# A fused top-k attention and two feed-forward stages on one core: GpSimd's elementwise work handed to ScalarE and VectorE, and another set of expert products beside the attention

## Chip, core and metric

One core of a Trainium2 chip runs the whole program. The metric is the device time of one execution in microseconds (us). The engines are called as the profile calls them: PE (TensorE's matmuls) and PEld (its weight loads), DVE (VectorE), ACT (ScalarE), POOL (GpSimd) and SP (SyncE, whose queue issues every DMA here). They run side by side, each through its own instructions in a fixed order, and wait for one another through semaphores.

## What is computed

```python
scores = (q @ k.T) / sqrt(64)            # 2 batches, 8 heads, 576 x 576
scores = where(scores >= 32nd largest of the row, scores, -1e9)
x  = softmax(scores) @ v                 # rearranged to 1152 x 512
h  = x @ w_in;  x1 = (h * sigmoid(h)) @ w_out          # 512 -> 2048 -> 512
P  = exp(x1 @ w_gate - max), 8 times scaled to row sums 1 and column sums N/8
out = sum over 8 experts e of P[:, e] * (relu(x1 @ w1[e]) @ w2[e])   # 512 -> 1024 -> 512
```

`w_in` and `w_out` arrive as 64-bit floats and are narrowed on the chip.

## The kernel before

The 1152 tokens are nine row tiles of 128. The attention is worked off as 72 score tiles (128 rows by 576 columns; 64 of one head, 8 that hold the last 64 rows of two heads). For each, `score_tile` (L283) makes the scores on PE, ACT copies them out of PSUM (L293), DVE finds the 32 largest with four `max` and three `match_replace` passes (L301, L307), ACT takes the exponential (L305), DVE masks and sums (`scalar_tensor_tensor`, L310) and inverts the sum (L312, L313), POOL multiplies the row by the inverse (L314), and PE transposes the result (L317, L319). `av` (L322) then multiplies by `v`.

Five groups of row tiles follow each other: tile 0; 1 and 2; 3 and 4; 5 and 6; 7 and 8. As soon as the attention of group 0, 1 or 2 is done, its rows go through the first feed-forward stage (m0, m1, m2) while DVE goes on with the attention of later groups. Tile 0 does so in `row_ffn` (L489): plain float32 matmuls with the activations as the stationary operand and 512 weight columns moving. Groups 1 and 2 do so in `ffn` and `step` (L428, L378), in 16 chunks of 128 hidden columns: each float32 operand is split in a high and a low part, and a product is three matmuls (`mm3`, L134). A chunk's weights are two 128x512 blocks, loaded by SP's queue and split by ACT and POOL in `load_split` (L527, the split itself at L127 and L128). A chunk's silu in `step` is: ACT takes tanh from PSUM (L403) and copies the PSUM tile (`hs`, L406), POOL multiplies and adds (L407, L408), makes the high part (L421) and the low part (L422). PE multiplies these by `w_out` two chunks later (depth 2).

What PE does besides, while the attention runs, is set by the table `FILL` (L24): expert products of row tiles whose x1 is known. After m0 these are experts 0 to 4 of tile 0 ("rows": `row_ffn` in float32, 8 hidden and 8 output matmuls and 8 transposes each). After m1 they are expert 0 of tiles 1 and 2 ("half": the second product in float32) and expert 1 of the same tiles (alternately "split" and "half"), and after m2 expert 0 of tiles 3 and 4 ("split"). Their results are parked in DRAM (`kept_y`).

After the attention, m3 takes the four tiles 5 to 8 together, then come the gate's logits, the eight rounds of scaling (on DVE), and the expert loop: `ORDER` says 7 down to 0, `left[e]` are the tiles of expert e that `FILL` has not done, and `units_of` (L783) cuts them in units of up to four tiles. `weighted` (L761) adds y times P to the accumulator.

The order of the instructions on each engine is not written by hand: the layer below builds a schedule from priorities (`tc.cur_priority`): attention first, then m0 to m2, `FILL` last. SBUF is handed out in stacks; where a new pool reuses memory, each of its tiles waits for the last use of what lay there. On one such stack `first_blocks` (L456) puts the 32 narrowed blocks of `w_in` and `w_out` (`wf`), one buffer each, and the rings of expert weights and of raw blocks (`raw`) come to lie on them when m0 is done.

Of the kernel before, what the change touches and what calls it, by code (L numbers as in the profile page):

```python
# [8 lines left out]
F32 = mybir.dt.float32  # L9
# [3 lines left out]
AF = mybir.ActivationFunctionType  # L13
ALU = mybir.AluOpType
# [3 lines left out]
P = 128  # L18
# [3 lines left out]


FILL = {  # L24
    0: [(e, [0], "rows") for e in range(5)],
    1: [(0, [1, 2], "half"), (1, [1, 2], "split+half")],
    2: [(0, [3, 4], "split")],
}

ORDER = [7, 6, 5, 4, 3, 2, 1, 0]  # L30
# [32 lines left out]
def topk_attention_moe_sinkhorn_kernel(  # L63
# [12 lines left out]
    nc = tc.nc  # L76
# [3 lines left out]
    DFF = w_in.shape[1]  # L80
# [3 lines left out]
    NTT = NT // P  # L84
# [3 lines left out]
    W = DM  # L88
# [26 lines left out]
    kept_y = {}  # L115
# [9 lines left out]
    def split(dH, dL, src, eng=nc.gpsimd):  # L125

        nc.scalar.activation(dH, src, AF.Copy)  # L127
        eng.tensor_sub(dL, src, dH.bitcast(F32))  # L128
# [154 lines left out]
    def score_tile(nm, qq, qL, kk, heads, cols):  # L283

        ps = ps_s.tile([P, 2, 512], F32, name=f"ps_{nm}", tag="s")

        for j in heads:
            for part, a in enumerate((qq, qL)):
                for hh in range(2):
                    nc.tensor.matmul(ps[:, hh, 0:SH], a[:, j, cols], kk[:, j, hh * SH : (hh + 1) * SH],  # L290
                                     start=j == heads[0] and part == 0, stop=j == heads[-1] and part == 1)
        s = sp.tile([P, S], F32, name=f"s_{nm}", tag="s", bufs=SB)
        nc.scalar.activation(s.rearrange("p (a c) -> p a c", a=2), ps[:, :, 0:SH], AF.Copy)  # L293
        w = sp.tile([P, S], F32, name=f"w_{nm}", tag="w")
        m8 = small.tile([P, TOPK], F32, name=f"m8_{nm}", tag="m8")
        sm = small.tile([P, 4], F32, name=f"sm_{nm}", tag="sm")
        e = sp.tile([P, S], F32, name=f"e_{nm}", tag="e")
        src = s
        for r in range(TOPK // 8):
            mr = m8[:, 8 * r : 8 * r + 8]  # L300
            nc.vector.max(mr, src)  # L301
            if r == 0:

                nc.vector.tensor_scalar(sm[:, 0:1], m8[:, 0:1], -SCALE, None, op0=ALU.mult)
                nc.scalar.activation(e, s, AF.Exp, scale=SCALE, bias=sm[:, 0:1])  # L305
            if r < TOPK // 8 - 1:
                nc.vector.match_replace(out=w, in_to_replace=mr, in_values=src, imm_value=-3e38)  # L307
                src = w

        nc.vector.scalar_tensor_tensor(s, s, m8[:, TOPK - 1 : TOPK], e, op0=ALU.is_ge, op1=ALU.mult,  # L310
                                       accum_out=sm[:, 1:2])
        nc.vector.tensor_scalar(sm[:, 2:3], sm[:, 1:2], 1e-9, None, op0=ALU.add)  # L312
        nc.vector.reciprocal(sm[:, 3:4], sm[:, 2:3])  # L313
        nc.gpsimd.tensor_scalar(s, s, sm[:, 3:4], 1.0, op0=ALU.mult, op1=ALU.mult)  # L314
        pt = ps_t.tile([P, 4, P], F32, name=f"pt_{nm}", tag="tr")
        for c in range(4):
            nc.tensor.transpose(pt[:, c, :], s[:, c * P : (c + 1) * P], ident)  # L317
        pt2 = ps_t.tile([P, P], F32, name=f"pt2_{nm}", tag="tr")
        nc.tensor.transpose(pt2, s[:, S - P : S], ident)  # L319
        return pt, pt2  # L320
# [57 lines left out]
    def step(pend, nm, xs, ys, wa, wb, first, last, silu, ph, pool, late=False, depth=2, done=None, half=False):  # L378


        N = len(ys) * P
        ph = ph[:, :N]
        hidden(ph, wa, xs)
        if half:

            gH = pool.tile([P, N], F32R, name=f"gH_{nm}", tag="gH", bufs=depth + 2).bitcast(F32)
            kept = tc.cur_priority
            tc.cur_priority = uid() * 100
            nc.scalar.activation(gH, ph, AF.Relu)
            tc.cur_priority = kept  # L390
            pend.append((ys, wb, gH, None, first, last, done))
            if len(pend) > depth:
                flush(pend)
            return
        gH = pool.tile([P, N], F32R, name=f"gH_{nm}", tag="gH", bufs=depth + 2)
        gL = pool.tile([P, N], F32R, name=f"gL_{nm}", tag="gL", bufs=depth + 2)
        kept = tc.cur_priority
        tc.cur_priority = uid() * 100
        if silu:

            g = hp.tile([P, W], F32, name=f"g_{nm}", tag="g")[:, :N]
            t = hp.tile([P, W], F32, name=f"t_{nm}", tag="t")[:, :N]
            nc.scalar.activation(t, ph, AF.Tanh, scale=0.5)  # L403
            if not late:
                hs = pool.tile([P, N], F32, name=f"hs_{nm}", tag="hs")
                nc.scalar.activation(hs, ph, AF.Copy)  # L406
                nc.gpsimd.tensor_mul(t, t, hs)  # L407
                nc.gpsimd.tensor_add(g, t, hs)  # L408
            else:
                nc.vector.scalar_tensor_tensor(g, t, 1.0, ph, op0=ALU.add, op1=ALU.mult)  # L410
            if late:
                nc.scalar.activation(gH, g, AF.Copy)
                nc.vector.tensor_sub(gL, g, gH.bitcast(F32))
        elif late:
            nc.scalar.activation(gH, ph, AF.Relu)  # L415
            nc.vector.scalar_tensor_tensor(gL, ph, 0.0, gH.bitcast(F32), op0=ALU.max, op1=ALU.subtract)  # L416
        else:
            g = hp.tile([P, W], F32, name=f"g_{nm}", tag="g")[:, :N]
            nc.scalar.activation(g, ph, AF.Relu)
        if not late:  # L420
            nc.gpsimd.tensor_scalar(gH, g, 1.0, 0.0, op0=ALU.mult, op1=ALU.add)  # L421
            nc.gpsimd.tensor_sub(gL, g, gH.bitcast(F32))  # L422
        tc.cur_priority = kept
        pend.append((ys, wb, gH, gL, first, last, done))
        if len(pend) > depth:
            flush(pend)
# [29 lines left out]
    def first_blocks():  # L456


        got = []
        for i in range(2 * DFF // P):  # L460
            tc.cur_priority = conv_at(i)
            F, part, c = i // (2 * NDC), i // NDC % 2, i % NDC
            r = slice(c * P, (c + 1) * P) if part == 0 else slice((F * NDC + c) * P, (F * NDC + c + 1) * P)
            cols = slice(F * W, (F + 1) * W) if part == 0 else slice(0, W)
            x = cvp.tile([P, W], F32, name=f"wf_{i}", tag=f"wf{i}", bufs=1)
            if w_in.dtype == F32:
                nc.sync.dma_start(x, (w_in, w_out)[part][r, cols])
            else:
                raw = cvp.tile([P, W], w_in.dtype, name=f"wfr_{i}", tag="raw")
                nc.sync.dma_start(raw, (w_in, w_out)[part][r, cols])  # L470
                narrow(x, raw, f"{i}")
            got.append(x)
            tc.cur_priority = keep_at(i)
            nc.sync.dma_start(kept_out[r] if part else kept_in[F, c], x)
        return lambda F: (got[2 * NDC * F : 2 * NDC * F + NDC], got[2 * NDC * F + NDC : 2 * NDC * (F + 1)])
# [142 lines left out]
    got = {0: load(units[0]), 1: load(units[1])}  # L618
    qs = turn(units[0], got[0])
    for u, unit in enumerate(units):  # L620
        g = unit[0]
# [18 lines left out]
        if g == 0:  # L640
# [6 lines left out]
            late = right.enter_context(tc.tile_pool(name="late", bufs=1, side="right", reuse_waits="tile"))  # L647
# [106 lines left out]

    last = {}
    left = {e: [tt for tt in range(NTT) if (e, tt) not in kept_y] for e in range(NE)}
    for e in ORDER:
        for tt in left[e]:
            last[tt] = e

    def weighted(e, tt, y):  # L761

        p_ = pr[:, tt, e : e + 1]
        if e == ORDER[0]:

            nc.scalar.activation(acc[:, tt, :], y, AF.Copy)
            return
        o = acc[:, tt, :]
        if last[tt] == e:
            o = x1p.tile([P, DM], F32, name=f"o_{tt}", tag="x1")  # L770
        nc.vector.scalar_tensor_tensor(o, y, p_, acc[:, tt, :], op0=ALU.mult, op1=ALU.add)
        if last[tt] == e:
            for p0, n, dst in out_rows(tt):
                nc.sync.dma_start(dst, o[p0 : p0 + n, :])
# [20 lines left out]
    for i, e in enumerate(ORDER):  # L795
        tc.cur_priority = (300 + i) * GAP
        if i == 1:
            while pend:
                flush(pend)
            for tt in range(NTT):  # L800
                nc.gpsimd.tensor_scalar(acc[:, tt, :], acc[:, tt, :], pr[:, tt, ORDER[0] : ORDER[0] + 1], 1.0,
                                        op0=ALU.mult, op1=ALU.mult)
            for ek, tt in kept_y:
                yk = x1p.tile([P, DM], F32, name=f"yk_{ek}_{tt}", tag="x1")
                nc.sync.dma_start(yk, kept_y[ek, tt])
                weighted(ek, tt, yk)
# [43 lines left out]
```

## Time and profile before

| | us |
|---|---|
| three timed runs: median (lowest to highest) | 1353.98 (1350.36 to 1355.71) |
| the profiled execution | 1354.5 |
| its span, first to last instruction | 1352.7 |
| PE busy in the span | 1247.3 (92%) |
| DVE busy | 734.8 (54%) |
| ACT busy | 515.8 (38%) |
| POOL busy | 446.0 (33%) |

The mean granted clock of PE is 0.962 of its full 2.4 GHz. Busy time counts an engine's instructions, not its waiting; matmuls overlap, so the time between the starts of two of them says more of their cost than their length does. The shares are means over stages that differ: in the stage up to about 545 us attention and feed-forward work lie side by side, and after it PE works through m3 and the expert loop.

### The profile page before, as it was taken

Reading aid. Unit: us, or ns where it says so; the run is one execution under the profiler, and the core shown is the slowest. Engines: PE = TensorE matmul, PEld = TensorE weight load, DVE = VectorE, ACT = ScalarE, POOL = GpSimd, SP = SyncE. Lnnn points to the kernel's source line nnn. Section 1 sums busy time; section 2 is a strip of 40 time slices with the busy share of each in tenths; the row PEclk is TensorE's granted clock in tenths of the full one; section 3 lists DMA queues with packets and bytes.
Section 4 is the critical chain, followed back from the end, with each engine's and each line's share of the span. In section 5 each row is a group of like instructions: output and inputs, shape, how many; then the busy total and the mean of one; then the engine's idle time right before and its main releaser. Section 6 shows DMA issues by size and latency. Waiting matters only on the chain.

```text
span 1352.7 us, 18344 instructions
## 1 busy us (share of the span) xinstructions
PE 1247.3 (92%) x6467; PEld 992.8 (73%) x6467; DVE 734.8 (54%) x1585; ACT 515.8 (38%) x1045; POOL 446.0 (33%) x469
## 2 busy tenths in 40 slices
PE   3568799998899868999999999999999999999998
PEld 2444455676677646888798898898888888888887
DVE  6999999999999936234435312322314223133232
ACT  4766445576557535444412311312213113122221
POOL 2654110599658997613101300200202002011110
PEclk7669899999999988999999999999999999999999
DMA  6998876654345332344302300301302104012210
GB/s 154 287 321 253 268 250 208 186 147 115 100 137 155 90 97 72 113 122 126 108 1 86 110 0 31 95 8 32 94 0 78 47 1 124 0 63 79 63 32 31
DMA packets 154700, 144.89 MB, mean 107 GB/s; under 512 B 34032, under 2 KB 113008, under 8 KB 154608
## 3 DMA queue, kind: packets, MB, share of 16 engines
q1 hardware_dynamic: 154608, 143.72, 35.5%
q8 instruction: 51, 0.84, 0.3%
q14 instruction: 41, 0.34, 0.1%
HBM read 119.03 MB, written 13.63 MB: 98 GB/s over the span
## 4 chain that ended last, share of the span: by engine, by line
PE 68%; DVE 14%; DMA 6%; issue 4%; POOL 4%; ACT 2%; SPq 1%; DVEq 0%; POOLq 0%; ACTq 0%
PE h L137 9%; PE h L136 9%; PE h L135 9%; PE y L135 8%; PE y L136 8%; PE y L137 8%; DVE m L301 5%; DVE w L307 5%; PE bank L497 3%; PE bank L504 2%; DMA wfr<-in_moe_w_in_dram 2%; DVE s L310 2%; PE bank L137 2%; PE bank L136 1%; PE bank L135 1%
## 5 line engine op out<-in xcount | busy, mean ns | idle before, releaser
L416 DVE SCALAR_TENSOR_TENSOR gL<-h,gH 128x512 fp32r<-128x512 f32 (+2 forms) x152 | 88.9, 585 | 311.2 <-ACT gH L415 311.0
L415 ACT ACTIVATE gH<-h 128x512 fp32r<-128x512 f32 (+2 forms) x152 | 78.1, 514 | 425.5 <-PE h L137 422.8
L128 POOL TENSOR_TENSOR wc<-raw,wc 128x512 fp32r<-128x512 f32 x40 | 52.0, 1300 | 452.3 <-ACT wc L127 445.8
L128 POOL TENSOR_TENSOR wa<-raw,wa 128x512 fp32r<-128x512 f32 x96 | 128.6, 1340 | 127.7 <-ACT wa L127 120.6
L301 DVE MAX8 m<-w 128x8 f32<-128x576 f32 x192 | 139.3, 744 | 0.2
L136 PE MATMUL h<-x1L,wc 128*128 128x512 f32 (+2 forms) x380 | 132.7, 349 | 0.0
L137 PE MATMUL h<-x1H,wc 128*128 128x512 f32 (+2 forms) x380 | 132.7, 349 | 0.0
L135 PE MATMUL h<-x1H,wc 128*128 128x512 f32 (+2 forms) x380 | 132.3, 348 | 0.0
L135 PE MATMUL y<-wc,gH 128*128 128x512 f32 x305 | 119.5, 392 | 0.0
L136 PE MATMUL y<-wc,gH 128*128 128x512 f32 x305 | 119.4, 391 | 0.0
L137 PE MATMUL y<-wc,gL 128*128 128x512 f32 x305 | 109.4, 391 | 0.0
L307 DVE MATCH_REPLACE8 w<-m,w 128x576 f32<-128x576 f32 x128 | 94.4, 738 | 0.0
L314 POOL TENSOR_SCALAR s<-s,sm 128x576 f32<-128x576 f32 x64 | 50.9, 795 | 120.5 <-DVE sm L313 78.9
L128 DVE TENSOR_TENSOR wc<-raw,wc 128x512 fp32r<-128x512 f32 x40 | 50.0, 1251 | 69.0 <-ACT wc L127 69.0
L127 ACT ACTIVATE wb<-raw 128x512 fp32r<-128x512 f32 x84 | 53.0, 631 | 71.7 <-PE y L137 23.6
L137 PE MATMUL h<-x1H,wa 128*128 128x512 f32 (+2 forms) x228 | 80.0, 351 | 0.0
L135 PE MATMUL h<-x1H,wa 128*128 128x512 f32 (+2 forms) x228 | 79.8, 350 | 0.0
L136 PE MATMUL h<-x1L,wa 128*128 128x512 f32 (+2 forms) x228 | 79.7, 350 | 0.0
L135 PEld LDWEIGHTS h<-x1H,wc 128*128 128x128 f32 x380 | 71.5, 188 | 10.5
L136 PEld LDWEIGHTS h<-x1L,wc 128*128 128x128 f32 x380 | 71.5, 188 | 10.4
L137 PEld LDWEIGHTS h<-x1H,wc 128*128 128x128 f32 x380 | 71.5, 188 | 8.3
L136 PE MATMUL y<-wb,gH 128*128 128x512 f32 x183 | 72.5, 396 | 0.0
(226 smaller groups left out, 3028.0 us busy)
## 6 DMA issues: line engine op xcount, KB each, us to landing
raw<-in_moe_w_dram SPq DMA_DIRECT2D x164, 256.0 KB, 3.0
raw<-kept_in SPq DMA_DIRECT2D x48, 256.0 KB, 2.9
raw<-kept_out SPq DMA_DIRECT2D x48, 256.0 KB, 2.7
wa<-in_moe_w_dram SPq DMA_DIRECT2D x20, 512.0 KB, 5.4
wb<-in_moe_w_dram SPq DMA_DIRECT2D x20, 512.0 KB, 4.9
wfr<-in_moe_w_in_dram SPq DMA_DIRECT2D x16, 512.0 KB, 5.4
wfr<-in_moe_w_out_dram SPq DMA_DIRECT2D x16, 512.0 KB, 5.8
kept_in<-wf SPq DMA_DIRECT2D x16, 256.0 KB, 5.3
```

Of the source, the lines that this page charges most:

```text
L127: nc.scalar.activation(dH, src, AF.Copy)
L128: eng.tensor_sub(dL, src, dH.bitcast(F32))
L135: nc.tensor.matmul(ps, wH, xH, start=first, stop=False)
L136: nc.tensor.matmul(ps, wH, xL, start=False, stop=False)
L137: nc.tensor.matmul(ps, wL, xH, start=False, stop=last)
L301: nc.vector.max(mr, src)
L307: nc.vector.match_replace(out=w, in_to_replace=mr, in_values=src, imm_value=-3e38)
L310: nc.vector.scalar_tensor_tensor(s, s, m8[:, TOPK - 1 : TOPK], e, op0=ALU.is_ge, op1=ALU.mult, accum_out=sm[:, 1:2])
L314: nc.gpsimd.tensor_scalar(s, s, sm[:, 3:4], 1.0, op0=ALU.mult, op1=ALU.mult)
L415: nc.scalar.activation(gH, ph, AF.Relu)
L416: nc.vector.scalar_tensor_tensor(gL, ph, 0.0, gH.bitcast(F32), op0=ALU.max, op1=ALU.subtract)
L497: nc.tensor.matmul(y, gT[:, c * P : (c + 1) * P], b[c], start=F == 0 and c == 0, stop=F == nF - 1 and c == NDC - 1)
```

## The change

It has four parts.

- In `score_tile`, ACT multiplies the row by the inverse of its sum (an `activation` with a scale per partition) in POOL's place.
- In `step`, silu is one `scalar_tensor_tensor` on DVE, (tanh + 1) times the PSUM tile, for every group; the copy `hs` and POOL's multiplication and addition are gone. The high part is made by ACT (`split`), the low part stays on POOL.
- `FILL` is another table: after m0 experts 0 to 5 of tile 0, after m1 expert 6 of tile 0 and expert 0 of tiles 1 and 2 ("split"), after m2 expert 7 of tile 0. The mode "half" is used no more. Ten products are parked where eleven were; the expert loop has tiles 1 to 8 in units of 4 and 4 for experts 7 to 1, and tiles 3 to 8 in units of 2 for expert 0. The accumulator of tile 0 begins with the first parked product.
- `first_blocks` hands out the 32 blocks in reverse, block 31 first.

```diff
 FILL = {
-    0: [(e, [0], "rows") for e in range(5)],
-    1: [(0, [1, 2], "half"), (1, [1, 2], "split+half")],
-    2: [(0, [3, 4], "split")],
+    0: [(e, [0], "rows") for e in range(6)],
+    1: [(6, [0], "rows"), (0, [1, 2], "split")],
+    2: [(7, [0], "rows")],
 }
@@ score_tile
-        nc.gpsimd.tensor_scalar(s, s, sm[:, 3:4], 1.0, op0=ALU.mult, op1=ALU.mult)
+        nc.scalar.activation(s, s, AF.Copy, scale=sm[:, 3:4])
@@ step
             nc.scalar.activation(t, ph, AF.Tanh, scale=0.5)
-            if not late:
-                hs = pool.tile([P, N], F32, name=f"hs_{nm}", tag="hs")
-                nc.scalar.activation(hs, ph, AF.Copy)
-                nc.gpsimd.tensor_mul(t, t, hs)
-                nc.gpsimd.tensor_add(g, t, hs)
-            else:
-                nc.vector.scalar_tensor_tensor(g, t, 1.0, ph, op0=ALU.add, op1=ALU.mult)
-            if late:
-                nc.scalar.activation(gH, g, AF.Copy)
-                nc.vector.tensor_sub(gL, g, gH.bitcast(F32))
+            nc.vector.scalar_tensor_tensor(g, t, 1.0, ph, op0=ALU.add, op1=ALU.mult)
+            split(gH, gL, g, nc.vector if late else nc.gpsimd)
...
             nc.scalar.activation(g, ph, AF.Relu)
-        if not late:
-            nc.gpsimd.tensor_scalar(gH, g, 1.0, 0.0, op0=ALU.mult, op1=ALU.add)
-            nc.gpsimd.tensor_sub(gL, g, gH.bitcast(F32))
+            split(gH, gL, g)
@@ first_blocks
-        got = []
+        got = [cvp.tile([P, W], F32, name=f"wf_{i}", tag=f"wf{i}", bufs=1) for i in reversed(range(nb))][::-1]
...
-            x = cvp.tile([P, W], F32, name=f"wf_{i}", tag=f"wf{i}", bufs=1)
+            x = got[i]
@@ weighted
-        if e == ORDER[0]:
+        if e == ORDER[0] and tt in left[e]:
             nc.scalar.activation(acc[:, tt, :], y, AF.Copy)
             return
+        if tt not in begun:
+            begun.add(tt)
+            nc.gpsimd.tensor_scalar(acc[:, tt, :], y, p_, 1.0, op0=ALU.mult, op1=ALU.mult)
+            return
```

What this makes of the order is shown at three places. In the rows, `wa`, `wb` and `wf` are weights, `x1H` and `x1L` the parts of x1, `bank` the PSUM banks of the work beside the attention.

The first is PE at the last three score tiles of the attention (`pt_4_1_3_...`). Before, expert 0 of tiles 3 and 4 lies around them (`gL_e_3`, then the next chunk's hidden matmuls):

```order
L317 MATMUL pt_1_3_1_0_6135<-ident,s_1_3_1_0_6116 128x128 x4
L319 MATMUL pt_4_1_3_1_0_6140<-ident,s_1_3_1_0_6116 128x128
L137 MATMUL bank_132<-wb_4615,gL_e_3_0_4637 128x512
L137 MATMUL bank_133<-wb_4615,gL_e_3_0_4637 128x512
L135 MATMUL bank_134<-x1H,wa_4670 128x256
L136 MATMUL bank_134<-x1L,wa_4670 128x256
```

With the change the float32 output matmuls of expert 7 (`gT_e_1`) end ahead of them, and the gate's logits follow (`wgH`, `wgL`):

```order
L319 MATMUL pt_4_1_3_0_1_5739<-ident,s_1_3_0_1_5715 128x128
L488 MATMUL bank_132<-wb_4496,gT_e_1_4516 128x512 x2
L488 MATMUL bank_132<-wb_4497,gT_e_1_4516 128x512 x2
L317 MATMUL pt_1_3_1_0_5767<-ident,s_1_3_1_0_5748 128x128 x4
L319 MATMUL pt_4_1_3_1_0_5772<-ident,s_1_3_1_0_5748 128x128
L571 MATMUL bank_134<-ident,lt_5822 128x8 x4
L317 MATMUL pt_1_3_1_1_5800<-ident,s_1_3_1_1_5781 128x128 x4
L319 MATMUL pt_4_1_3_1_1_5805<-ident,s_1_3_1_1_5781 128x128
L135 MATMUL bank_134<-x1H,wgH 8x128
```

Behind the last score tile stood 60 hidden and 36 output matmuls of expert 0 and all the logits of tiles 0 to 4; of these only the 12 logit matmuls of tile 4 are left there.

The second place is a chunk of m2. Before, POOL has its silu in four steps among the scalings of score tiles (L314) and the weight splits (L128):

```order
L421 TENSOR_SCALAR gH_m_1_4029<-g_m_1_4031 128x256
L408 TENSOR_TENSOR g_m_2_4064<-t_m_2_4065,hs_m_2_4067 128x256
L128 TENSOR_TENSOR wb_4119<-raw_4124,wb_4119 128x512
L422 TENSOR_TENSOR gL_m_1_4030<-g_m_1_4031,gH_m_1_4029 128x256
L421 TENSOR_SCALAR gH_m_2_4062<-g_m_2_4064 128x256
L407 TENSOR_TENSOR t_m_3_4104<-t_m_3_4104,hs_m_3_4106 128x256
L128 TENSOR_TENSOR wa_4196<-raw_4198,wa_4196 128x512
L314 TENSOR_SCALAR s_1_1_0_1_5775<-s_1_1_0_1_5775,sm_1_1_0_1_5779 128x576
```

With the change DVE has it in one step among the passes over score tiles:

```order
L404 SCALAR_TENSOR_TENSOR g_m_1_3936<-t_m_1_3937,bank_134 128x256
L310 SCALAR_TENSOR_TENSOR s_1_0_1_0_5276,sm_1_0_1_0_5280<-s_1_0_1_0_5276,m_4_1_0_1_0_5279,e_1_0_1_0_5281 128x576
L307 MATCH_REPLACE w_1_1_0_0_5376<-m_4_1_1_0_0_5377,s_1_1_0_0_5374 128x576
L301 MAX m_4_1_0_1_1_5312<-w_1_0_1_1_5311 128x8
L301 MAX m_4_1_1_0_1_5410<-s_1_1_0_1_5407 128x8
L312 TENSOR_SCALAR sm_1_0_1_0_5280<-sm_1_0_1_0_5280 128x1
L301 MAX m_4_1_1_0_0_5377<-w_1_1_0_0_5376 128x8
L307 MATCH_REPLACE w_1_0_1_1_5311<-m_4_1_0_1_1_5312,w_1_0_1_1_5311 128x576
L404 SCALAR_TENSOR_TENSOR g_m_2_3966<-t_m_2_3967,bank_134 128x256
```

The scaling and the high part are on ACT, and seven to ten DVE rows lie between one chunk's silu and the next one's. The PSUM half `bank_134` is now given back by DVE, not by ACT's copy.

The third is SP's queue where the first raw blocks of m1 are loaded. Before, and then with the change:

```order
L529 DMA raw_1968<-kept_in 128x4x128 [waits DMAHW2_49]
L529 DMA raw_1972<-kept_out 128x512 [waits DMAHW3_49]
L529 DMA raw_2001<-kept_in 128x4x128 [waits DMAHW4_49]
L529 DMA raw_2005<-kept_out 128x512 [waits DMAHW5_49]
L529 DMA raw_2034<-kept_in 128x4x128 [waits DMAHW6_49]
```

```order
L520 DMA raw_2020<-kept_in 128x4x128 [waits DMAHW2_49,PE_49]
L520 DMA raw_2024<-kept_out 128x512 [waits DMAHW3_49]
L520 DMA raw_2050<-kept_in 128x4x128 [waits DMAHW4_49]
L520 DMA raw_2054<-kept_out 128x512 [waits DMAHW5_49]
L520 DMA raw_2080<-kept_in 128x4x128 [waits DMAHW6_49]
```

The first of them now also waits for PE: it lies on block 28, whose matmul is one of the last four of m0.

## Rows read from the trace of the kernel before

**Rows 1.** Stretches: length, busy PE, PEld, DVE, ACT, POOL, clock, DMA share, GB/s.

```profile
150.00:270.00 120.00, 117.11 (x560) 68.68 (x557) 112.56 (x288) 60.02 (x128) 29.63 (x35) 0.99 0.75 236
270.00:450.00 180.00, 162.60 (x1063) 127.08 (x1062) 179.53 (x440) 113.81 (x256) 145.62 (x161) 0.99 0.45 129
450.00:545.00 95.00, 73.93 (x407) 58.38 (x405) 54.46 (x131) 47.07 (x104) 87.26 (x103) 0.89 0.30 87
700.00:1345.00 645.00, 645.00 (x3125) 544.15 (x3124) 193.77 (x295) 142.36 (x264) 79.38 (x65) 1.00 0.17 50
```

**Rows 2.** Waits of DVE, 450 to 545 us: total, times, longest.

```profile
DVE xL L132 <- ACT xH L131: 29.1, 1, 29.1
```

**Rows 3.** Groups on POOL, 270 to 545 us: busy us, mean ns | idle before.

```profile
L128 POOL TENSOR_TENSOR wa<-raw,wa 128x512 fp32r<-128x512 f32 x49 | 67.3, 1373 | 7.7 <-ACT wa L127 5.3 <-DMA wb<-in_moe_w_dram 1.7 <-POOL wb L128 0.7
L128 POOL TENSOR_TENSOR wb<-raw,wb 128x512 fp32r<-128x512 f32 x39 | 52.4, 1344 | 4.6 <-ACT wb L127 4.6
L314 POOL TENSOR_SCALAR s<-s,sm 128x576 f32<-128x576 f32 x34 | 27.0, 794 | 25.8 <-DVE sm L313 18.2 <-PE bank L137 5.9 <-DMA wb<-in_moe_w_dram 1.7
...
L407 POOL TENSOR_TENSOR t_m<-t_m,hs_m 128x256 f32<-128x256 f32 x30 | 23.6, 788 | 0.0
L408 POOL TENSOR_TENSOR g_m<-t_m,hs_m 128x256 f32<-128x256 f32 x30 | 22.9, 765 | 0.0
L421 POOL TENSOR_SCALAR gH_m<-g_m 128x256 fp32r<-128x256 f32 x31 | 14.2, 458 | 0.0
```

**Rows 4.** Chain that ended last, 450 to 515 us: start, us, what.

```profile
502.62 1.23 POOL wa L128
...
508.78 0.69 POOL gL_m L422
509.52 1.12 PE bank L137 x2
```

**Rows 5.** Chain, rest of the span: m0's end, float32 matmuls, the last `av`.

```profile
132.78 3.44 PE bank L497 x8
...
176.88 3.44 PE bank L504 x8
...
545.38 2.31 PE pav L327 x20
```

**Rows 6.** Timeline of PE, split matmuls: start, length.

```profile
664.38 0.34 PE L135 MATMUL h<-x1H,wc 128*128 128x384 f32 x1
...
666.33 0.34 PE L137 MATMUL h<-x1H,wc 128*128 128x384 f32 x1
...
700.78 0.28 PE L135 MATMUL h<-x1H,wc 128*128 128x256 f32 x1
...
701.50 0.39 PE L135 MATMUL y<-wb,gH 128*128 128x512 f32 x1
...
703.60 0.28 PE L135 MATMUL h<-x1H,wc 128*128 128x256 f32 x1
...
834.20 0.39 PE L135 MATMUL h<-x1H,wc 128*128 128x512 f32 x1
...
836.92 0.39 PE L135 MATMUL y<-wc,gH 128*128 128x512 f32 x1
```

**Rows 7.** Line 310 alone, 150 to 270 us, then 300 to 450: ns min/median/max.

```profile
L310 DVE SCALAR_TENSOR_TENSOR s<-s,m,e x14: 793/811/1152, 149.3 to 259.8; 128x576 f32<-128x576 f32 x14
...
L310 DVE SCALAR_TENSOR_TENSOR s<-s,m,e x23: 797/1280/1943, 305.8 to 447.3; 128x576 f32<-128x576 f32 x23
```

**Rows 8.** Groups by form, whole span: busy us, mean ns | idle before.

```profile
L416 DVE SCALAR_TENSOR_TENSOR gL<-h,gH 128x256 fp32r<-128x256 f32 x48 | 20.4, 424 | 92.3 <-ACT gH L415 92.3
...
L403 ACT ACTIVATE t_m<-bank 128x256 f32<-128x256 f32 x32 | 12.3, 383 | 18.2 <-POOL g_m L408 11.9 <-PE bank L137 6.1
```

**Rows 9.** Groups on ACT, 270 to 545 us, same columns.

```profile
L305 ACT ACTIVATE e<-s,sm 128x576 f32<-128x576 f32 x34 | 26.5, 780 | 28.2 <-DVE s L310 27.9
```

**Rows 10.** Timeline of SP's queue, 118 to 200 us: start, length, issue.

```profile
137.85 0.59 SPq L529 DMA_DIRECT2D raw<-kept_in  x1
```

More of the change, by code (lines that the diff above doesn't have):

```diff
@@ L456, in first_blocks @@
     def first_blocks():
-        got = []
-        for i in range(2 * DFF // P):
+        nb = 2 * DFF // P
+        got = [cvp.tile([P, W], F32, name=f"wf_{i}", tag=f"wf{i}", bufs=1) for i in reversed(range(nb))][::-1]
+        for i in range(nb):
             tc.cur_priority = conv_at(i)
@@ L471, in first_blocks @@
                 narrow(x, raw, f"{i}")
-            got.append(x)
             tc.cur_priority = keep_at(i)
@@ L756, in topk_attention_moe_sinkhorn_kernel @@
     left = {e: [tt for tt in range(NTT) if (e, tt) not in kept_y] for e in range(NE)}
-    for e in ORDER:
-        for tt in left[e]:
-            last[tt] = e
+    for e, tt in [*kept_y] + [(e, tt) for e in ORDER for tt in left[e]]:
+        last[tt] = e
+    begun = set(left[ORDER[0]])
     def weighted(e, tt, y):
         p_ = pr[:, tt, e : e + 1]
-        if e == ORDER[0]:
+        if e == ORDER[0] and tt in left[e]:
             nc.scalar.activation(acc[:, tt, :], y, AF.Copy)
+            return
+        if tt not in begun:
+            begun.add(tt)
+            nc.gpsimd.tensor_scalar(acc[:, tt, :], y, p_, 1.0, op0=ALU.mult, op1=ALU.mult)
             return
@@ L799, in topk_attention_moe_sinkhorn_kernel @@
                 flush(pend)
-            for tt in range(NTT):
+            for tt in left[ORDER[0]]:
                 nc.gpsimd.tensor_scalar(acc[:, tt, :], acc[:, tt, :], pr[:, tt, ORDER[0] : ORDER[0] + 1], 1.0,
```

## The prediction

> **What bounds the kernel now.** I read the stretches first. From 700 us to the end of the expert loop PE is busy 645.0 of 645.0 us [rows 1]: there only the number of PE's instructions counts, and no engine's help. So the time is made of the moment at which the attention ends, plus PE's work behind it. Up to 545 us the picture changes from stretch to stretch. From 150 to 270 us PE is busy 117.1 of 120 and DVE 112.6: both are nearly full. From 270 to 450 DVE is full (179.5 of 180) and PE still has 162.6. From 450 to 545 neither is: DVE 54.5 of 95, PE 73.9, but POOL 87.3. The waits and the chain say why: DVE stood 29.1 us for a single operand, the high part of an attention output [rows 2], and the chain runs through POOL until PE goes on at 509.5 [rows 4]. PE's order has chunks of m2 ahead of the score tiles it needs, and those chunks wait for POOL's silu and POOL's weight splits. POOL was not slow there alone: it fell behind from 270 us on, where its work amounts to 145.6 + 87.3 = 232.9 us in 275.
>
> I call the stretch from 270 to 545 us "the stage". In it DVE was idle 275 - (179.5 + 54.5) = 41.0 us and PE 275 - (162.6 + 73.9) = 38.5 us. What the change can gain lies in these two numbers.
>
> **PE's work.** Prices are distances between starts. A float32 matmul of 512 columns leaves two records of 3.44/8 = 0.43 us (four matmuls are issued where a row counts eight) [rows 5], so 0.86. A split matmul takes 0.72/6 = 0.12 at 256 columns, 1.95/11 = 0.177 at 384, 2.72/12 = 0.227 at 512 for a hidden one, 2.10/9 = 0.233 for an output one in small units [rows 6]. From these:
> - an expert on one tile in rows: 16 x 0.86 + 8 transposes at no more than 0.12 = 14.7;
> - a chunk of two tiles: 12 x 0.12 + 6 x 0.233 = 2.84 split, 1.44 + 2 x 0.86 = 3.16 half; of three: 12 x 0.177 + 9 x 0.233 = 4.22; of four: 24 x 0.227 = 5.45.
>
> Beside the attention the change takes away 8 x 3.16 + 4 x (3.16 + 2.84) + 8 x 2.84 = 72.0 and adds 3 x 14.7 + 8 x 2.84 = 66.8: -5.2. In the expert loop, per chunk, experts 7, 6 and 5 go from 12.51 to 10.90 each (-4.83), expert 1 from 8.29 to 10.90 (+2.61), expert 0 gets one more unit of two (+2.84): +0.62, times 8 chunks +5.0. In all PE's work stays as it was; what moves is its place. The order shows that 60 hidden and 36 output matmuls of expert 0 (60 x 0.12 + 36 x 0.233 = 15.6) and 12 logit matmuls (2.8) no longer stand behind the last score tile. So behind it PE has 15.6 + 2.8 - 5.0 = 13.4 us less, and in the stage 15.6 + 2.8 - 5.2 = 13.2 more.
>
> **The other engines in the stage.** POOL loses the scalings 27.0, the silu steps 23.6 + 22.9, the high parts 14.2 [rows 3], and 88 weight splits become 80 (64 of m1 and m2 and 16 of expert 0) at (67.3 + 52.4)/88 = 1.36, which is 11. That leaves 232.9 - 98.7 = 134 us, half of the stage where it was 85%, so POOL no longer sets the pace.
>
> DVE gains 32 silu steps. Its nearest row, the same operation on a PSUM tile of 128x256, took 424 ns [rows 8]: +13.6. It may get some back at line 310: 811 ns in the median where POOL was 25% busy, 1280 ns where it was 81% [rows 1, 7]. For some 34 tiles that is between 0 and 34 x 0.47 = 16; I take half, 8, because POOL's load falls to half and not to a quarter. DVE's need: 234.0 + 13.6 - 8 = 239.6 (231.6 to 247.6). The Trainium skill (SBUF — State Buffer, "Who interferes with whom") holds that a DVE operation with two SBUF inputs and a GpSimd operation that reads SBUF exclude each other for a whole instruction; the two medians of line 310 agree with it. By that rule the loss shrinks only with POOL's share, from 85% to 51%, so that 16 x 51/85 = 9.6 stays, and DVE's need would be 241.2 in place of 239.6.
>
> ACT takes over the scaling. Its nearest row is the exponential of the same 128x576 tile, SBUF to SBUF with an operand per partition: 780 ns [rows 9]; 34 x 0.78 = 26.5. The high part replaces the copy `hs` at equal size. ACT had 113.8 + 47.1 = 160.9 us, and gets to about 190. It has room, but its queue is in order: where a scaling waits for DVE, the tanh and the weight splits behind it wait too.
>
> **Edits at nothing.** The reversed blocks let the first raw load wait for one of the last four matmuls of m0. These ended at 132.78 + 3.44 = 136.2 [rows 5], and the load was issued at 137.85 [rows 10], behind a queue that issues without a break; the margin is 1.6 us. Without it the loads behind it, expert weights among them, slip by as much as m0 does: 0 to 3 us. One parked product less and the accumulator's other start lie under a full PE.
>
> **How long the stage gets.** PE needs 236.5 + 13.2 = 249.7. The granted clock was 0.89 from 450 to 545 us [rows 1], a mean of 2.4 GHz and some 1.2 GHz, in a stretch in which PE kept waiting for POOL; up to 0.11 x 73.9 = 8 us come back if these waits go, and I take 4: 245.7. Both engines are then nearly equally loaded. They were so from 150 to 270 us, where PE reached 97.6%: 252 us. With DVE full, from 270 to 450, PE reached 90.3%: 272 us. I take the middle, **262 us** in place of 275; DVE is then at 91%.
>
> Behind the stage there were 1352.7 - 545 = 807.7 us; now 807.7 - 13.4, and about 3 more because no expert work covers the last `av` (2.31 [rows 5]) and its copies: 797.3. Span: 270 + 262 + 797.3 = 1329.3. The profiled execution took 1354.5, 1.8 over its span and 0.5 over the median; I keep the 1.8: **1331 us**, 1.7% less than the median of 1354.0. Something like 0.5% (1347 to 1361) is what a measurement can tell from no change.
>
> **Rivals.**
> - *POOL was all that held both engines*: PE runs the stage full in 250 us, or 242 with the whole clock: 1319, at best 1311. For it: PE at 97.6% beside rows work, and more of the work beside the attention is now rows, which needs neither POOL nor DVE. Against it: m1 and m2 now lie closer together in the rest of the attention. Chance 0.2.
> - *The wait changes its name*: DVE keeps its 41.0 idle us, since PE's order, now as before, has a long run of m2 chunks ahead of a score tile, now waiting for ACT and DVE. Stage 239.6 + 41.0 = 280.6, time 1350. For it: the 29.1 us came from that order. Against it: POOL's 98.7 us are really gone. Chance 0.17.
> - *Slower: DVE and PE wait for each other in silu.* The half bank of a chunk is now given back only when DVE reaches its silu step; PE then needs 12 x 0.12 = 1.44 for the next hidden product and ACT 0.38 for tanh [rows 8], and DVE's next silu step stands at the head of its queue until both are done. If each of the 32 chunks makes DVE wait for all of it, that is 32 x 1.82 = 58 idle us: stage 298, time 1367. It decides from 52 idle us on, 1.6 per chunk (1361). For it: DVE's queue did stand for one operand [rows 2]. Against it: two half banks, and seven to ten DVE rows between two silu steps in the order. Chance 0.13.
>
> **How the numbers follow.** The forecast has 0.5: the stage between 252 and 272 us, 1321 to 1341. The range 1316 to 1353 takes in most of the first rival and the second one and leaves out the slower one. Faster by over 0.5%: the forecast, the first rival and a sixth of the second, 0.72; within 0.5%: most of the second and some of the third, 0.15; slower 0.13.
>
> **What would show it.** Right: POOL under 60% in the stage; the wait of about 29 us for an attention output gone or under 15; the last `av` near 532 us and not 545; PE idle in the stage under 20 us; line 310 near 1.0 us; 645 us of full PE in the loop as before, and about 5 longer. Wrong: DVE idle over 40 us in the stage, with silu steps or ACT's scalings as what it waits for; or a wait for weights in the rows work, which now goes on longer and had a DMA share of 0.75.

## The result and the profile after

The changed kernel takes 1336.69 us in the median of four runs (1335.55 to 1342.04); the kernel before, beside it, 1354.85 (1350.36 to 1356.95). The ratio is 0.9878, with an interval of 0.9841 to 0.9915: 1.2% faster. The profiled execution took 1342.04 us, its span is 1340.3; a second set of runs (first experiment) gave 1337.35, so this profile lies about 5 us over the median.

Stretches of the changed kernel, columns as in [rows 1]; the last one ends with the full loop:

```profile
150.00:270.00 120.00, 116.19 (x492) 65.67 (x493) 104.74 (x267) 62.60 (x128) 0.20 (x1) 0.96 0.74 237
270.00:450.00 180.00, 162.66 (x1029) 124.88 (x1027) 167.54 (x426) 132.93 (x290) 99.53 (x87) 0.97 0.51 148
450.00:545.00 95.00, 84.94 (x506) 61.32 (x505) 83.70 (x211) 65.30 (x137) 43.44 (x39) 1.00 0.44 134
700.00:1330.00 630.00, 629.93 (x2863) 517.88 (x2862) 187.15 (x252) 134.30 (x240) 82.47 (x65) 1.00 0.17 51
```

POOL fell from 232.9 to 99.5 + 43.4 = 143.0 us in the stage, 52% of it. PE is idle 27.4 us there where it was 38.5, DVE 23.8 where it was 41.0. The stretch from 150 to 270 us got worse, though: DVE has 104.7 there, and had 112.6 [rows 1].

DVE's wait for the attention output of [rows 2], 29.1 us, is gone. The one wait for such an output that is left from 450 to 545 us is for the very last:

```profile
DVE xL L132 <- ACT xH L131: 2.2, 1, 2.2
```

Groups on POOL and on ACT from 270 to 545 us (columns of [rows 3]); of the work in [rows 3], the weight splits are left on POOL, with the low parts, and the scaling is on ACT at about the length of the exponential [rows 9]:

```profile
L128 POOL TENSOR_TENSOR wa<-raw,wa 128x512 fp32r<-128x512 f32 x43 | 56.2, 1307 | 58.9 <-ACT wa L127 50.0 <-PE pq L252 6.3 <-issue 1.9
L128 POOL TENSOR_TENSOR wb<-raw,wb 128x512 fp32r<-128x512 f32 x40 | 55.0, 1378 | 20.4 <-ACT wb L127 20.4
L128 POOL TENSOR_TENSOR gL_m<-g_m,gH_m 128x256 fp32r<-128x256 f32 x32 | 26.7, 833 | 23.7 <-ACT gH_m L127 20.3 <-DMA wa<-in_moe_w_dram 2.5 <-DMA qq<-qH 0.8
```

```profile
L314 ACT ACTIVATE s<-s,sm 128x576 f32<-128x576 f32 x36 | 27.8, 774 | 5.6 <-DVE sm L313 5.3 <-DVE sm L304 0.3
```

The silu steps on DVE (ns min/median/max) answer to L416 in [rows 8]:

```profile
L404 DVE SCALAR_TENSOR_TENSOR g_m<-t_m,bank x32: 392/401/423, 306.1 to 508.2; 128x256 f32<-128x256 f32 x32
```

And the last `av`, at 545.38 in [rows 5]:

```profile
L327 PE MATMUL pav<-aT,vn x20: 379/379/430, 541.7 to 543.7; 128*64 128x256 f32 x20
```

So the wait is gone and POOL is relieved as the change meant, but the attention ends only 3.6 us earlier. Behind the last `av` there are 1340.3 - 541.7 = 798.6 us where there were 807.4. Following the score tiles by the start of their mask (L310) shows where the rest went: tile 28 came at 230.2 us and not at 215.8, tile 37 at 299.2 and not at 278.3. The attention ran up to 26 us late in its middle, then passed the place where it had stood for 29.1 us without stopping (tiles counted in the order of these starts).

### The profile page after: what moved, and what is told of

The parts are those of the page before. It is cut to its first block, busy times and chain, and to the rows that moved or that the text cites. A ratio compares the mean times of both kernels' runs of the same rounds, so it can differ in the third digit from the quotient of the medians.

```text
span 1340.3 us, 17430 instructions
## 1 busy us (share of the span) xinstructions
PE 1245.1 (93%) x6155; PEld 962.7 (72%) x6155; DVE 737.7 (55%) x1601; ACT 551.5 (41%) x1083; POOL 301.5 (22%) x265
## 4 chain that ended last, share of the span: by engine, by line
PE 74%; DVE 10%; DMA 8%; ACT 4%; SPq 2%; issue 2%; POOL 0%; DVEq 0%; ACTq 0%; POOLq 0%
PE h L135 10%; PE h L136 10%; PE h L137 10%; PE y L136 9%; PE y L135 9%; PE y L137 9%; PE bank L495 4%; PE bank L488 4%; DVE m L301 4%; DVE w L307 3%; DMA wfr<-in_moe_w_out_dram 2%; PE pav L327 2%; DVE s L310 1%; PE bank L135 1%; PE bank L136 1%
## 5 line engine op out<-in xcount | busy, mean ns | idle before, releaser
L407 ACT ACTIVATE gH<-h 128x512 fp32r<-128x512 f32 (+1 forms) x136 | 76.1, 560 | 442.9 <-PE h L137 433.0
L408 DVE SCALAR_TENSOR_TENSOR gL<-h,gH 128x512 fp32r<-128x512 f32 (+1 forms) x136 | 87.4, 643 | 307.2 <-ACT gH L407 307.2
L128 POOL TENSOR_TENSOR wc<-raw,wc 128x512 fp32r<-128x512 f32 x40 | 54.2, 1357 | 430.5 <-ACT wc L127 430.3
L128 POOL TENSOR_TENSOR wa<-raw,wa 128x512 fp32r<-128x512 f32 x80 | 105.5, 1319 | 181.3 <-ACT wa L127 172.4
L136 PE MATMUL h<-x1L,wc 128*128 128x512 f32 (+1 forms) x340 | 127.3, 374 | 0.0
L135 PE MATMUL h<-x1H,wc 128*128 128x512 f32 (+1 forms) x340 | 127.1, 374 | 0.0
L137 PE MATMUL h<-x1H,wc 128*128 128x512 f32 (+1 forms) x340 | 127.1, 374 | 0.0
L128 DVE TENSOR_TENSOR wc<-raw,wc 128x512 fp32r<-128x512 f32 x40 | 51.9, 1300 | 60.2 <-ACT wc L127 60.2
L137 PE MATMUL h<-x1H,wa 128*128 128x512 f32 (+1 forms) x204 | 76.5, 375 | 0.0
L136 PE MATMUL h<-x1L,wa 128*128 128x512 f32 (+1 forms) x204 | 76.4, 374 | 0.0
L135 PE MATMUL h<-x1H,wa 128*128 128x512 f32 (+1 forms) x204 | 76.2, 374 | 0.0
L136 PE MATMUL y<-wb,gH 128*128 128x512 f32 x186 | 73.9, 397 | 0.0
L135 PE MATMUL y<-wb,gH 128*128 128x512 f32 x186 | 73.4, 395 | 0.0
L135 PEld LDWEIGHTS h<-x1H,wc 128*128 128x128 f32 x340 | 64.0, 188 | 12.7
L136 PEld LDWEIGHTS h<-x1L,wc 128*128 128x128 f32 x340 | 64.0, 188 | 12.4
L137 PEld LDWEIGHTS h<-x1H,wc 128*128 128x128 f32 x340 | 64.0, 188 | 11.9
```

The lines of the kernel that those rows point to most:

```text
L135: nc.tensor.matmul(ps, wH, xH, start=first, stop=False)
L136: nc.tensor.matmul(ps, wH, xL, start=False, stop=False)
L137: nc.tensor.matmul(ps, wL, xH, start=False, stop=last)
```

## Experiments

All twelve were timed beside the kernel before (ratio to it, 95% interval). Two columns are read from the traces: the start of the mask of score tile 28, and of the last `av`.

| kernel | median us | ratio | tile 28 | last `av` |
|---|---|---|---|---|
| before | 1354 | 1 | 215.8 | 545.3 |
| 1 changed kernel again | 1337.35 | 0.9883 [0.9867, 0.9899] | 229.3 | 539.6 |
| 2 relief alone (scaling on ACT, silu on DVE) | 1325.43 | 0.9789 [0.9774, 0.9804] | 226.5 | 522.9 |
| 3 table alone | 1361.95 | 1.0061 [1.0042, 1.0080] | 216.9 | 557.2 |
| 4 changed, blocks in old order | 1337.46 | 0.9874 [0.9856, 0.9892] | 229.7 | 539.1 |
| 5 scaling alone | 1337.86 | 0.9882 [0.9866, 0.9899] | 228.4 | 530.5 |
| 6 silu alone | 1322.59 | 0.9775 [0.9751, 0.9798] | 216.9 | 519.1 |
| 7 changed, expert 5 behind m1 | 1328.23 | 0.9810 [0.9791, 0.9829] | 229.4 | 527.5 |
| 8 relief, old table without "half" | 1320.62 | 0.9756 [0.9738, 0.9774] | 227.4 | 529.7 |
| 9 changed, scaling on POOL | 1335.07 | 0.9857 [0.9841, 0.9874] | 218.1 | 534.1 |
| 10 silu alone, without "half" | 1318.81 | 0.9738 [0.9721, 0.9755] | 218.7 | 524.5 |
| 11 as 10, one product in rows less | 1320.50 | 0.9747 [0.9727, 0.9767] | 217.4 | 520.7 |
| 12 as 10, scaling on ACT from group 3 on | 1322.43 | 0.9767 [0.9750, 0.9784] | 220.6 | 519.0 |

**1. The changed kernel again**, no edit.

> The changed kernel once more, for a second profile. Theory T1 (the gain is the change of place: 13 us of PE work moved ahead of an attention end that hardly moved): last av again between 538 and 544 us, time 1334 to 1340. Rival T2 (the relief of POOL shortens the attention, and the first profile, 5 us above the median, hid it): last av near 535, rest behind it 798.

T1's numbers came: last `av` at 539.6, 798.0 us behind it. But this run cannot say why it is so.

**2. The relief alone.** The kernel before with

```diff
-        nc.gpsimd.tensor_scalar(s, s, sm[:, 3:4], 1.0, op0=ALU.mult, op1=ALU.mult)
+        nc.scalar.activation(s, s, AF.Copy, scale=sm[:, 3:4])
...
-                nc.gpsimd.tensor_mul(t, t, hs)
-                nc.gpsimd.tensor_add(g, t, hs)
+            nc.vector.scalar_tensor_tensor(g, t, 1.0, ph, op0=ALU.add, op1=ALU.mult)
+            split(gH, gL, g, nc.vector if late else nc.gpsimd)
```

> The kernel before with only the scaling on ACT and silu on DVE; its old table and blocks. T1: the 29 us wait goes, but the attention comes later in its middle, so the last av moves by less than 6 us; the rest behind it stays near 807 less what the order leaves there: 1345 to 1354. T2: the relief is the gain, last av at 530 or earlier: 1335 to 1342. Rival T3 (the relief itself delays the attention, by the scaling on ACT and the silu on DVE): score tile 37 begins its mask 15 us or more later than before (278.3), as in the changed kernel (299.2).

T1 falls: the relief alone is faster than the whole change, with the last `av` 22 us earlier than before, although tile 37 did come 16 us late (294.0), as T3 said. T2 had the last `av` right and was 10 us too long in the time. The stage of kernel 2, 270 us to its last `av` (columns of [rows 1]):

```profile
270.00:522.90 252.90, 232.99 (x1527) 184.37 (x1523) 244.47 (x624) 191.21 (x415) 146.40 (x130) 0.99 0.45 129
```

DVE is busy 244.5 of 252.9 us there (97%) and PE 233.0 (92%): with POOL relieved, it is DVE that is nearly full.

**3. The table alone**, and **4. the changed kernel with the blocks in their old order** (`got.append(x)` in the loop again).

```diff
-    0: [(e, [0], "rows") for e in range(5)],
-    1: [(0, [1, 2], "half"), (1, [1, 2], "split+half")],
-    2: [(0, [3, 4], "split")],
+    0: [(e, [0], "rows") for e in range(6)],
+    1: [(6, [0], "rows"), (0, [1, 2], "split")],
+    2: [(7, [0], "rows")],
```

> The kernel before with only the new table and what the expert loop needs for it; POOL keeps scaling and silu. T1: the rows stretch with experts 5 and 6 delays the attention: score tile 37 at 290 or later; POOL still loaded (over 200 us from 270 to 545), last av 545 to 555, rest behind it 795 to 799: 1342 to 1354. T2: nothing gained, 1352 or more. T3: tile 37 stays near 278.

> The changed kernel with the 32 narrowed blocks in their old order. All theories: 0 to 3 us from the first load of m1's weights, so 1334 to 1340 beside 1337. If the reversed order is what makes the attention late in its middle, score tile 37 comes back from 299 towards 278 and the time falls below 1330.

The order of the blocks makes no difference (1337.46 beside 1337.35). The table alone makes the kernel slower, by 8.0 us, as T2 said; tile 37 came at 285.3 us, short of T1's 290 and over T3's 278. DVE's wait for the attention output grew from 29.1 to 35.0 us (waits of kernel 3, 440 to 560 us), and the chain of kernel 3 runs through POOL up to 520 us:

```profile
DVE xL L132 <- ACT xH L131: 35.0, 1, 35.0
```

```profile
509.80 1.27 POOL wa L128
...
516.00 1.22 POOL wb L128
...
519.68 0.69 POOL gL_m L422
520.37 0.04 issue
520.42 0.74 PE bank L137 x2
```

Kernels 2 and 4 differ in the table, with what the expert loop needs for it, and in nothing else: it costs 12.0 us in the medians, 15.4 in the two profiles. The stretch from the start to the last `av`, of kernel 2 and then of kernel 4 (columns of [rows 1]):

```profile
0.00:522.90 522.90, 447.00 (x2460) 314.87 (x2460) 479.31 (x1214) 363.41 (x754) 211.16 (x197) 0.96 0.62 187
```

```profile
0.00:539.10 539.10, 455.39 (x2390) 310.30 (x2390) 482.12 (x1219) 359.31 (x740) 192.15 (x179) 0.95 0.64 193
```

Up to the last `av`, PE is busy 8.4 us longer with the new table and idle 83.7 us instead of 75.9: 16.2 later. Behind it, the transposes of x1 that end m3 separate m3 from the logits and the loop. The first and the last group of them, in kernel 2 and in kernel 4:

```profile
629.37 1.15 PE L550 MATMUL bank<-ident,x 128*128 128x128 f32 x8
...
632.18 0.66 PE L550 MATMUL y_m<-ident,x 128*128 128x128 f32 x4 [0.32 <-ACT x L547]
```

```profile
634.41 1.15 PE L550 MATMUL bank<-ident,x 128*128 128x128 f32 x8
...
637.22 0.66 PE L550 MATMUL y_m<-ident,x 128*128 128x128 f32 x4 [0.32 <-ACT x L547]
```

From the last `av` to the first of them it is 106.5 us and 95.3: 11.2 less, since nothing of expert 0 is left there, and little of the logits. From the last of them to the end of the span (1322.1 and 1337.5) it is 689.9 and 700.3: 10.4 more. The whole is 16.2 - 11.2 + 10.4 = 15.4. The 10.4 is the one product more that the loop has: its experts work 62 pairs of expert and tile, where they worked 61. All fourteen traces agree: this distance is 689.9 to 691.4 us in the seven kernels that leave 61 pairs to the loop (before, 2, 5, 6, 8, 10, 12), and 700.1 to 701.7 in the seven that leave 62. A hidden matmul of 512 columns in kernel 4's loop:

```profile
1001.96 0.39 PE L135 MATMUL h<-x1H,wc 128*128 128x512 f32 x1
...
1004.76 0.39 PE L135 MATMUL y<-wc,gH 128*128 128x512 f32 x1
```

Between the two rows start 12 matmuls, 2.80/12 = 0.233 us each. A tile takes 24 x 128 columns of this in a chunk, which is 6 x 0.233 = 1.40 us, and in 8 chunks 11.2. A tile in rows costs 15: three products more in kernel 4 added 45.1 us of distances between starts ahead of the last `av`. So each product that the new table does in rows instead of in the loop costs PE nearly 4 us.

**5. The scaling alone** and **6. silu alone**: each one half of the diff of kernel 2.

> The kernel before with only the softmax scaling on ACT. Theory R1 (POOL's load counts, whatever it is made of: 27 of the 98.7 us that it loses): a third of what the relief gave, some 9 of 28 us: 1342 to 1348. Rival R2 (only what stands in the chain of a chunk counts, and that is silu, not the scaling): 1349 to 1354. Rival R3 (the scaling on ACT is what delays the attention's middle): score tile 28 begins its mask at 225 us or later (before 215.8, relief 226.5).

> The kernel before with only silu on DVE and its high part on ACT; POOL keeps the scaling. R1: two thirds of the relief's gain: 1333 to 1337. R2: all of it, 1323 to 1328, with line 310 slower than in the relief kernel since POOL still scales (1.0 us or more in its mean). R3: score tile 28 at 216 to 219, as before.

Each part works by itself, 16.9 and 32.1 us in the medians of that set, and together they gave 28.5 (kernel 2): the scaling adds nothing to silu. R1 misses both times, kernel 5 by 4 us and kernel 6 by 10: POOL's load is not a price per us. R2 is right for kernel 6, within half a us, and 11 us off for kernel 5: not silu alone matters. Either part pulls POOL out of the way; silu does it better. The DVE step that waited 29.1 us before waited 0.2 in kernel 5 and not at all in kernel 6 (DVE's timeline):

```profile
496.48 0.76 DVE L132 TENSOR_TENSOR xL<-pav,xH 128x256 fp32r<-128x256 f32 x2 [0.21 <-ACT xH L131]
```

```profile
485.72 0.73 DVE L132 TENSOR_TENSOR xL<-pav,xH 128x256 fp32r<-128x256 f32 x2
```

R3 holds: tile 28 comes 11 to 14 us late in every kernel with ACT's scaling in the early groups, and at most 5 in every one without, as the table of runs shows. The mask of that tile is the last start in each row (ns min/median/max), in kernel 2, then in kernel 6:

```profile
L310 DVE SCALAR_TENSOR_TENSOR s_h<-s_h,m_h,e_h x2: 817/818/820, 218.2 to 226.5; 128x576 f32<-128x576 f32 x2
```

```profile
L310 DVE SCALAR_TENSOR_TENSOR s_h<-s_h,m_h,e_h x1: 817/817/817, 216.9 to 216.9; 128x576 f32<-128x576 f32 x1
```

ACT is not slow: the scaling started 0.0 to 2.2 us after the inverse in kernel 2 from 150 to 270 us. It is PE's order that changed. PE's timeline of kernel 2 from the last transpose (L319) of the 20th score tile to that of the 21st; L487 and L494 are the float32 rows:

```profile
182.92 0.27 PE L319 MATMUL pt<-ident,s 128*128 128x128 f32 x1
...
183.56 3.60 PE L487 MATMUL bank<-wb,gT_e 128*128 128x512 f32 x8
...
187.42 3.60 PE L494 MATMUL bank<-wa,x1F 128*128 128x512 f32 x8
190.95 2.38 PE L327 MATMUL pav<-aT,vn 128*64 128x256 f32 x20
...
194.27 3.60 PE L487 MATMUL bank<-wb,gT_e 128*128 128x512 f32 x8
...
198.14 3.60 PE L494 MATMUL bank<-wa,x1F 128*128 128x512 f32 x8
201.58 0.27 PE L319 MATMUL pt<-ident,s 128*128 128x128 f32 x1
```

and of kernel 6 between the same two:

```profile
177.26 0.27 PE L319 MATMUL pt<-ident,s 128*128 128x128 f32 x1
...
177.81 3.60 PE L494 MATMUL bank<-wa,x1F 128*128 128x512 f32 x8
181.33 2.38 PE L327 MATMUL pav<-aT,vn 128*64 128x256 f32 x20
...
184.67 3.60 PE L487 MATMUL bank<-wb,gT_e 128*128 128x512 f32 x8
...
188.54 3.60 PE L494 MATMUL bank<-wa,x1F 128*128 128x512 f32 x8
191.97 0.27 PE L319 MATMUL pt<-ident,s 128*128 128x128 f32 x1
```

With the scaling on ACT four blocks of float32 rows stand between the two tiles, without it three. The schedule puts filler work ahead of the score tile, here 3.4 us, and the lag grows from 5.7 to 9.6 us. PE is nearly full in both (119.4 and 118.6 of the 120 us from 150 to 270), so no wait shows it.

**7. Expert 5 behind m1**, **8. the relief with "split" throughout.**

```diff
-    0: [(e, [0], "rows") for e in range(6)],
-    1: [(6, [0], "rows"), (0, [1, 2], "split")],
+    0: [(e, [0], "rows") for e in range(5)],
+    1: [(5, [0], "rows"), (6, [0], "rows"), (0, [1, 2], "split")],
```

```diff
-    1: [(0, [1, 2], "half"), (1, [1, 2], "split+half")],
+    1: [(0, [1, 2], "split"), (1, [1, 2], "split")],
```

> The changed kernel with the rows of expert 5 behind m1 instead of ahead of it; the same work. Against the relief alone the table cost 12 us: PE was 8.4 us longer busy and 7.8 us longer idle up to the last av. Theory S1 (the idle time comes from m1 being pushed back by the longer rows): PE idle up to the last av falls from 84 to 76 to 79, time 1328 to 1333. Rival S2 (it comes with the rows wherever they stand): idle stays over 82, 1335 to 1339. In both the busy time stays, so it is not faster than the relief alone (1325).

> The relief alone, and in the old table expert 0 and 1 of tiles 1 and 2 in split mode throughout (no half): 12 chunks of 3.16 us become 2.84, 3.8 us less PE work; POOL gets 12 splits more (16 us), ACT 12. If PE's work counts: 1320 to 1323. If DVE sets the end of the attention (it was full from 270 us on): last av stays at 521 to 525 and the time at 1321 to 1326. If POOL or ACT delay the chunks again: 1328 or more.

Kernel 7, start to last `av`:

```profile
0.00:527.50 527.50, 449.85 (x2391) 307.00 (x2391) 482.06 (x1220) 358.23 (x742) 189.50 (x179) 0.93 0.66 198
```

527.5 - 449.9 = 77.6 us idle: S1 holds. The first matmul of m1 starts at 254.2 us, where it started at 300.6 in kernel 4 (251.3 in kernel 2), and moving one product in rows behind m1 gives 9 us back (1328.2 beside 1337.4). The loop's 10.4 us stay, so it is no faster than kernel 2. In kernel 8 PE's work counts, as forecast: 1320.6 beside 1325.4 for the 3.8 us, with intervals that touch. The last `av`, at 529.7, is later than the 521 to 525 expected if DVE set the end: all of the expert work now lies ahead of it (95.7 us from it to the transposes of m3, where kernel 4 has 95.3).

**9. The changed kernel with the scaling on POOL**, and **10. silu alone with "split" throughout**: edits as above.

> The changed kernel with the softmax scaling back on POOL (silu stays on DVE). Theory V1 (ACT's scaling helps nothing where silu no longer fills POOL, and makes the attention late at score tiles 22 to 28 through PE's order): tile 28 begins its mask at 215 to 219 us instead of 230, time 1331 to 1336. Rival V2 (with the new table the scaling on ACT pays): 1338 or more.

> Silu on DVE, scaling on POOL, the old table with split instead of half. Beside the same with the scaling on ACT (1320.6): V1: 1316 to 1319, tile 28 at 215 to 219. V2 (12 splits more make POOL, 183 us of 249 with silu alone, the bound again): 1322 or more, POOL over 85% from 270 us to the last av.

V1 holds in both. The scaling on POOL is 1.8 to 2.8 us faster in three pairs (6 and 2, 9 and 1, 10 and 8); the intervals of each pair overlap, the direction is the same three times. Kernel 10 is the fastest of all, 1.3% below the changed kernel, though POOL is busy 213 of 254 us in its stage:

```profile
270.00:524.50 254.50, 231.58 (x1574) 193.33 (x1574) 241.32 (x605) 180.37 (x407) 213.45 (x199) 1.00 0.47 132
```

**11. One product in rows less** (`range(4)`), and **12. the scaling on ACT from group 3 on** (`if nm[0] in "012"` for POOL, else ACT).

> As e10 with one product in rows less beside the attention (experts 0 to 3 of tile 0). The product costs PE 15.0 us in rows and 11.3 in the loop; the loop gets 11.3 longer, and the attention must end at least as much earlier to make up for it. If DVE sets its end, it can win only what DVE was idle from 150 to 270 us, 5 us: 1 to 7 us slower than e10. If PE's order with the rows in it sets the end: 4 us faster than e10.

> As e10 with the scaling on POOL for groups 0 to 2 and on ACT for groups 3 and 4. If the scaling on ACT costs only where POOL stands idle anyway: 0 to 4 us faster than e10, tile 28 as there. If POOL's scaling is covered in the late groups too: within 1.5 us of e10.

Kernel 11 is 1.7 us slower than 10, inside what was expected, but the intervals overlap: inconclusive by the time. Its trace says what it trades: the last `av` 3.8 us earlier, and 11.3 us more from the end of m3 to the end. Kernel 12 missed both expectations: 3.6 us slower than 10, with intervals that just touch. Its last `av` is the earliest of all (519.0), but more expert work lies behind it. Why the schedule comes out so was not tried.

## Why the prediction was right, and where not

The time was right, 1331 for 1336.7, within the range. So was the main part of the mechanism: POOL's work in PE's order was what held the attention, and kernels 2, 5 and 6 show it by taking it away. That the sum came so near is partly luck. The relief was worth 28.5 us by itself (kernel 2) and the table cost 12.0 of them, where the forecast had 23 for both and the table for nothing; two errors made up for each other.

- **"In all PE's work stays as it was" failed.** The step in it is the loop's "+5.0": it measured 10.4 (kernels 2 and 4). I had priced all of a unit of four at 2.72/12 = 0.227 a matmul, from one short stretch of starts, and the output matmuls of the smaller units at 0.233 from another, so that a unit of four came to 5.45 us a chunk. That was the choice of the stretch and not a difference between hidden and output matmuls: kernel 4's stretch has 0.233 for hidden ones, and over the whole of its loop the starts of either kind lie 0.23 apart. At one price for all, 0.233, the unit is 24 x 0.233 = 5.6. Two sums of some 680 us were compared, the new one has four units of four more in each chunk, and an error of 3% in their price came to nearly 5 us. Counting pairs of expert and tile, 62 for 61, at 11.2 comes near it at once. With it, the table's work is not -0.2 but about 8.4 - 11.2 + 10.4 = 7.6.
- **"How long the stage gets", 262, failed at its start.** The sum took the attention to stand at 270 us where it stood before. Tile 37 came 21 us late, and DVE's need of 239.6 us measured 251.2, of which about 8 is work that the stretch from 150 to 270 had done before. About 14 of the 21 are the scaling on ACT through PE's order (kernel 9, with the scaling back on POOL, has tile 37 at 285.0). At the end less of it is left: kernel 9's last `av` is 5.5 us ahead of kernel 1's, its time 2.3. The rows of expert 5 ahead of m1 cost the rest of the stage 9 us more (kernel 7). Without the table the stage is 522.9 - 270 = 252.9 us (kernel 2), with it 271.7. I had the relief too small and the table for free. The 4 us for the clock are not against the traces: the mean granted clock of the stage was 0.96 before and 0.98 after.
- **The rest, 797.3 us,** measured 798.6, by two errors: the old table had more behind the last `av` than I took away (114.7 us became 95.0 from there to the transposes of m3, 19.7 less where I had 18.4 - 3 = 15.4), and the loop got 10.4 and not 5.0 longer.
- **Prices of single instructions** were near: scaling 774 ns for 780, silu 401 for 424; so were POOL's need, 143 us for 134, and the reversed blocks, which cost nothing (kernel 4).
- **Line 310** was near 1.0 us (mean 1009 ns from 270 to 450). That is no proof of the reason given, a loss in proportion to POOL's share: in the kernels of the last section it was 1223 ns where POOL was busy 66% of the stretch and 994 where it was 76%. The rule of the Trainium skill (SBUF — State Buffer, "Who interferes with whom"), that such a pair of instructions excludes each other, is not against this; what failed is my reading of it as a loss in proportion to POOL's share.
- **The rivals.** "The wait changes its name" falls: DVE was idle 23.8 us, not 41.0. "Slower" falls: DVE's waits for tanh are few (4.9 us in three waits from 440 to 560 us), and kernel 6, which has the whole round trip, is faster than the forecast. "POOL was all" falls too. Kernel 2's stage of 252.9 us is near the 250 that the rival gave, but that 250 held 13.2 us of PE's work from the new table, which kernel 2 does not have, and PE does not run full in it (19.9 us idle): DVE does.
- **What would show it**: POOL under 60%, the wait gone, the loop full: right. The last `av` near 532 and PE idle under 20: wrong (541.7 and 27.4), and these two pointed to the stage.

What stays open is why the schedule puts other blocks ahead of a score tile when one step moves from POOL to ACT; the order shows that it does, and its builder was not varied.

## What to carry to other kernels

A change of several parts is worth timing by parts: here one part gave more than all (1322.6 us for 1336.7), and one cost 12. Work moved beside a bound stage is not free if it is done in a dearer form there; price it by the same unit on both sides, here us per tile and expert (15 in rows, 11.2 in the loop). And where a scheduler makes the order, an operation given to another engine moves the filler work of a third one: read how far the critical stage has come at several points, not only its end.

## What the runs showed of the hardware that was not expected

Two float32 inputs on DVE (L310) beside a busy POOL: groups from 270 to 450 us (busy us, mean ns), in kernels 9, 12, 8 and 2, where POOL was busy 66, 76, 71 and 56% of the stretch:

```profile
L310 DVE SCALAR_TENSOR_TENSOR s<-s,m,e 128x576 f32<-128x576 f32 x23 | 28.1, 1223 | 0.0
```

```profile
L310 DVE SCALAR_TENSOR_TENSOR s<-s,m,e 128x576 f32<-128x576 f32 x24 | 23.9, 994 | 0.0
```

```profile
L310 DVE SCALAR_TENSOR_TENSOR s<-s,m,e 128x576 f32<-128x576 f32 x23 | 27.0, 1174 | 0.0
```

```profile
L310 DVE SCALAR_TENSOR_TENSOR s<-s,m,e 128x576 f32<-128x576 f32 x24 | 22.9, 955 | 0.0
```

Over all fourteen traces the mean is 955 to 1021 ns where POOL was busy 54 to 57%, and 994 to 1283 where it was busy 66 to 86%, without following the share within either group. Nor does it go with whether POOL still scales: kernel 8 has all its scalings on ACT and 1174 ns, kernel 10 has them on POOL, which is busy 85%, and 1109. So POOL's busy share alone does not price such an instruction; what does was not tried.

In kernel 5 one L310 took 8.21 us, ten times its shortest (0.79 in [rows 7]), while POOL ran without a gap:

```profile
282.02 8.21 DVE L310 SCALAR_TENSOR_TENSOR s_h<-s_h,m_h,e_h 128x576 f32<-128x576 f32 x1
```

```profile
281.79 1.27 POOL L128 TENSOR_TENSOR wa<-raw,wa 128x512 fp32r<-128x512 f32 x1
283.02 1.29 POOL L128 TENSOR_TENSOR wb<-raw,wb 128x512 fp32r<-128x512 f32 x1
...
288.53 0.71 POOL L422 TENSOR_TENSOR gL_m<-g_m,gH_m 128x256 fp32r<-128x256 f32 x1
289.23 0.40 POOL L421 TENSOR_SCALAR gH_m<-g_m 128x256 fp32r<-128x256 f32 x1
```

Nine POOL instructions follow each other there, the last of them ends at 289.6, and L310 at 290.2, as if it had run when POOL first paused. This is one instruction of one profile: every other L310 of the fourteen traces took 1.94 us or less. By the Trainium skill (SBUF — State Buffer, "Who interferes with whom") the one that comes first holds the shared ports for a whole instruction. The row agrees that the other waits, but here it waited for several.
